# Loading wo in 112 partitions, with the last four heads' rows in small loads of their own, in a decode kernel with a 1 GB cache

## The chip, the cores and the metric

The kernel runs on one core of a Trainium2 chip. The metric is the device time of one execution in microseconds (us). A profile of one execution goes with it; its span is counted from the first to the last instruction, and the time of that same execution is a little longer than the span.

## The reference, cut to what matters

One token `x` of 512 numbers goes through attention over a cache of 65,536 positions with 32 heads of 128, and through a small gated network; a gate `g` mixes the two.

```python
q = (x @ wq).reshape(B, Sq, H, Dh).transpose(0, 2, 1, 3)          # H = 32, Dh = 128
p = softmax(einsum("bhqd,bhkd->bhqk", q, k_cache) * Dh ** -0.5)   # Sk = 65536
o = einsum("bhqk,bhkd->bhqd", p, v_cache)
a = o.transpose(0, 2, 1, 3).reshape(B, Sq, H * Dh) @ wo           # wo: 4096 x 512
b = (silu(x @ w_gate) * (x @ w_up)) @ w_down                      # w_gate: 512 x 1792
out = g * a + (1 - g) * b                                         # g = sigmoid(sum(x * gate_w))
```

All tensors are bf16. Each head's K and V take 16 MB each; `wo` takes 4 MB, 128 rows of 1 KB for each head.

## The kernel before

One big tile, `mem`, has 184 slots of 1 KB in each of 128 partitions, and nearly everything that is loaded goes through it: K and V in halves of 8 MB (64 KB in each partition), the weights at the start, and `wo` and the last head's V at the end. All large loads are issued by SP on one queue (lines 201 to 244), in an order written out by hand, each after a wait that tells that its slots are free: `ktdone` counts VectorE's transposes of K (16 for each head), `pvdone` counts TensorE's quarters of the products with V (4 for each head, ahead by 4).

For each head VectorE transposes K in 16 blocks (lines 399 and 406), TensorE multiplies them by q (line 452), ScalarE takes the exponential (line 301), VectorE rearranges the probabilities into `pb` (line 340), and TensorE multiplies them by V one head later (line 500). The result of head h is scaled and turned into column h of `oTn` (line 295), already multiplied by the gate.

The last head and the output are done apart, and this is what the change touches.

- V of head 31 comes in eight pieces, listed in `tail` (line 59): slot, first row, number of rows. The pieces have 4096, 4096, 4096, 2048, 1024, 512, 256 and 256 KB. `piece(n)` (line 506) waits for one and adds its products, with V as the stationary operand, to a column of `psW`.
- `wo` is loaded whole (line 235) into slots 64 to 95, as 128 partitions of 32 KB, each with 32 rows of `wo`. Partition p holds rows 32p to 32p + 31, a quarter of a head. Heads 0 to 30 are rearranged to fit: VectorE copies `oTn` into `amat` (line 414), one product with `bmat` (line 521) puts them into `psQ`, VectorE copies that to `oR` (line 417), and 32 products (line 526) add to the row `psY`, which already holds the gated network's result. That row is copied (line 419) and spread over four partitions of `psZ` (line 532).
- Head 31 is last. Its 128 rows of `wo` are loaded once more as 128 partitions of 1 KB (line 244), behind all of V, into slot 96 (`WO31`), when TensorE has read the last of head 30's V (`pvdone` at 4H). When `psW` is complete, VectorE writes it, scaled, on the diagonal of `w4` (line 422), and four products (line 544) add the head to `psZ`. ScalarE casts it and issues the output (lines 308 and 310).

SP's order at the end is thus: `wo`, the eight pieces (waits before pieces 0, 1 and 2), the wait for `pvdone` at 4H, head 31's rows. TensorE's order is: piece 0, the products of `wo`, piece 1, the four products into `psZ`, pieces 2 to 7, head 31's four products.

Of the kernel before, what the change touches and what calls it, by code (L numbers as in the profile page):

```python
# [5 lines left out]
P = 128  # L6
# [4 lines left out]
ALU = mybir.AluOpType  # L11
ACT = mybir.ActivationFunctionType
BF16 = mybir.dt.bfloat16
# [7 lines left out]
def bass_gated_mix__mha_block_cached__swiglu_ffn__decode_kernel(  # L21
# [13 lines left out]
    _, H, S, Dh = A_k_cache.shape  # L35
    D = A_wq.shape[0]
# [11 lines left out]
    KA, KZ, VA, VZ, V0 = 32, 0, 120, 96, 96  # L48
# [9 lines left out]

    tail = [(32, 0, 128), (0, 128, 128), (V0 + 24, 256, 128), (V0 + 64, 384, 64),
            (V0 + 80, 448, 32), (V0 + 56, 480, 16), (V0 + 60, 496, 8), (V0 + 62, 504, 8)]  # L60
    WO31 = V0

    with ExitStack() as ctx:
        def sb(name, shape, dt):
            return ctx.enter_context(nc.sbuf_tensor(name, shape, dt))
# [4 lines left out]
        def sem(name):  # L70
            return ctx.enter_context(nc.semaphore(name))
# [3 lines left out]
        psY = psum("psY", [P, 512], F32)  # L75
# [3 lines left out]
        psW = psum("psW", [P, 512], F32)  # L79
        psZ = psum("psZ", [P, 512], F32)  # L80
# [19 lines left out]
        oTn = sb("oTn", [P, H], BF16)  # L100
        amat = sb("amat", [P, H, 4], BF16)
        bmat = sb("bmat", [P, 32], BF16)
        oR = sb("oR", [P, 32], BF16)
        w4 = sb("w4", [P, 4, 4], BF16)
        fin = sb("fin", [P, 128], BF16)

        def at(kb, n):
            return mem[:, kb * KB:kb * KB + n]
# [5 lines left out]
        yrow = kt[:, 0, 0:512].bitcast(F32)  # L114
        mxs, amx, nbias, rsum, Lt, Li, LiG = (sm[:, i:i + 1] for i in range(7))

        names = ("x", "gw", "wq", "wg", "wu", "wd", "ka0", "ka", "kz", "va", "vz", "wo", "w31")
        d = {n: sem("d_" + n) for n in names}
        dt_ = [sem(f"d_t{i}") for i in range(len(tail))]
        s_ones = sem("s_ones")  # L120
# [27 lines left out]
        pvdone = sem("pvdone")  # L148
# [15 lines left out]
        s_yr = sem("s_yr")  # L164
        s_w = sem("s_w")
        s_w4 = sem("s_w4")
        s_z4 = sem("s_z4")
        s_fin = sem("s_fin")
        s_out = sem("s_out")
# [6 lines left out]
            "wg": B_w_gate.rearrange("(p c) f -> p (c f)", c=Dc),  # L176
            "wu": B_w_up.rearrange("(p c) f -> p (c f)", c=Dc),
            "wd": B_w_down.rearrange("(p c) n -> p (c n)", c=FC),
            "wo": A_wo.rearrange("(p j) n -> p (j n)", p=P),
        }  # L180
        w31_dram = A_wo.rearrange("(h d) n -> h d n", d=Dh)[H - 1]
        WQ, WG, WU, WD, WO = V0, 0, 14, V0 + 64, 64
        wq_ap = at(WQ, Dc * H * Dh).rearrange("p (c n) -> p c n", c=Dc)
        wg_ap = at(WG, Dc * F).rearrange("p (c m j) -> p c m j", c=Dc, j=FC)
        wu_ap = at(WU, Dc * F).rearrange("p (c m j) -> p c m j", c=Dc, j=FC)
        wd_ap = at(WD, FC * D).rearrange("p (c n) -> p c n", c=FC)
        wo_ap = at(WO, 32 * D).rearrange("p (j n) -> p j n", j=32)
        w31_ap = at(WO31, D).rearrange("p (c n) -> p c n", c=4)
        ktb = [kt[:, b, :].bitcast(BF16).rearrange("p (j r m e) -> p j r m e", j=2, r=NG, e=2) for b in range(2)]

        def place(kind, h, z):
# [9 lines left out]
        @block.sync  # L201
        def _(sp):
            def load(kind, h, z):
                cache = A_k_cache if kind == "k" else A_v_cache
                sp.dma_start(at(place(kind, h, z), HR * Dh), kv_dram(cache, h)[z]).then_inc(d[kind + "az"[z]], 16)

            def weights(n, kb):
                src = w_dram[n]
                sp.dma_start(at(kb, src.shape[1]), src).then_inc(d[n], 16)

            weights("wq", WQ)
            weights("wg", WG)
            weights("wu", WU)
            weights("wd", WD)
            half = HR // 2 * Dh
            for n in range(2):
                sp.dma_start(at(KA + 32 * n, half), kv_dram(A_k_cache, 0)[0][:, n * half:n * half + half]).then_inc(
                    (d["ka0"], d["ka"])[n], 16)
            sp.wait_ge(s_q, 1)
            load("k", 0, 1)  # L220
            for h in range(1, H):
                sp.wait_ge(ktdone, 2 * NP * h - 3 if h > 1 else NP)
                load("k", h, 0)
                if h == 1:
                    sp.wait_ge(ktdone, 2 * NP - 3)
                    sp.wait_ge(s_b, 1)
                else:
                    sp.wait_ge(pvdone, 4 * h - 1)
                load("v", h - 1, 0)
                sp.wait_ge(ktdone, 2 * NP * h + NP // 2)  # L230
                load("k", h, 1)
                sp.wait_ge(pvdone, 4 * h + 1)
                load("v", h - 1, 1)
            sp.wait_ge(ktdone, 2 * NP * H - NP)
            weights("wo", WO)
            src = A_v_cache[0, H - 1].rearrange("(b p r) d -> b p (r d)", b=2, p=P)
            need = {0: (ktdone, 2 * NP * H - 3), 1: (ktdone, 2 * NP * H), 2: (pvdone, 4 * H - 1)}
            for n, (kb, r0, nr) in enumerate(tail):
                if n in need:
                    sp.wait_ge(*need[n])  # L240
                b, o = divmod(r0, HR)
                sp.dma_start(at(kb, nr * Dh), src[b][:, o * Dh:(o + nr) * Dh]).then_inc(dt_[n], 16)  # L242
            sp.wait_ge(pvdone, 4 * H)
            sp.dma_start(at(WO31, D), w31_dram).then_inc(d["w31"], 16)

        @block.gpsimd
        def _(pool):
# [66 lines left out]
        def _(dve):  # L314
# [62 lines left out]
            for g in range(4):  # L377
                last = nc.vector.tensor_copy(qd[32 * g:32 * g + 32, :, :, g],
                                             psQ[32 * g:32 * g + 32, :, 0:H].rearrange("p e h -> p h e"))
# [11 lines left out]
            with nc.vector.Fori(1, H) as i:  # L391
                n = i * (2 * NP)
# [3 lines left out]
                for c, u in enumerate(k_order[0]):  # L396
                    dve.wait_ge(qkdone, n + (c - 1))  # L397
                    src = at(KA + 8 * u, PR * Dh).bitcast(U32)
# [4 lines left out]
                for c, u in enumerate(k_order[1]):  # L403
                    dve.wait_ge(qkdone, n + (NP + c - 1))  # L404
                    src = at(KZ + 8 * u, PR * Dh).bitcast(U32)
# [5 lines left out]
            link(nc.vector.tensor_tensor(LiG, Li, gcol[:, 0:1], ALU.mult))  # L411
            dve.wait_ge(s_otn, H - 1)
            for q in range(4):
                last = nc.vector.tensor_copy(amat[32 * q:32 * q + 32, 0:H - 1, q], oTn[32 * q:32 * q + 32, 0:H - 1])
            last.then_inc(s_A, 1)
            dve.wait_ge(s_R, 1)
            nc.vector.tensor_copy(oR[:], psQ[:, 0, 0:32]).then_inc(s_oR, 1)
            dve.wait_ge(s_y, 1)
            nc.vector.tensor_copy(yrow[0:1, :], psY[0:1, :]).then_inc(s_yr, 1)
            dve.wait_ge(s_w, 1)  # L420
            diag = w4[:].rearrange("p a b -> p (a b)")[:, 0:16:5]
            nc.vector.tensor_scalar(diag, psW[:, 0:1].to_broadcast([P, 4]), LiG, None, ALU.mult).then_inc(s_w4, 1)  # L422

        @block.tensor
        def _(pe):
# [3 lines left out]
            for c in range(Dc):  # L429
                last = nc.tensor.matmul(psM[:, c:c + 1], xv[:, c, :], ones[0:1, 0:1], start=True, stop=True)  # L430
# [3 lines left out]
            for h in range(H):  # L434
                for c in range(Dc):
                    last = nc.tensor.matmul(psM[:, 128 + h:129 + h], wq_ap[:, c, h * Dh:(h + 1) * Dh],  # L436
                                            xTb[:, c:c + 1], start=(c == 0), stop=(c == Dc - 1))
# [3 lines left out]
            for je in range(4):  # L441
                last = nc.tensor.matmul(psQ[:, je, 0:H], sel[:, je, :], qTb[:], start=True, stop=True)
# [28 lines left out]
            for j in range(FC):  # L471
                last = nc.tensor.matmul(psY[0:1, :], guT[:, j:j + 1], wd_ap[:, j, :],
                                        start=(j == 0), stop=False)
# [3 lines left out]
            def turn(h):  # L477
                pe.wait_ge(s_or, h)
                for i in range(4):
                    last = nc.tensor.matmul(psT[:, 0:1], orow[0:4, i * Dh:(i + 1) * Dh], unit[0:4, i:i + 1],  # L480
                                            start=(i == 0), stop=(i == 3))
                last.then_inc(s_pt, 1)

            nc.tensor.sem_inc(pvdone, 4)
            with nc.tensor.Fori(0, H) as i:
                n = i * (2 * NP)
                pe.wait_ge(s_qc, i + 1)
                for z in range(2):
# [3 lines left out]
                    with nc.tensor.If(i > 0):  # L492
# [5 lines left out]
                        for part, rows in enumerate(v_order[z]):  # L498
                            for m, r in enumerate(rows):
                                last = nc.tensor.matmul(psO[0:4, :], pb[:, 256 * z + r:256 * z + r + 4],  # L500
                                                        vt[:, r * Dh:(r + 4) * Dh],
                                                        start=(z == 0 and part == 0 and m == 0),
                                                        stop=(z == 1 and part == 1 and m == len(rows) - 1))
                            last.then_inc(pvdone, 1)

            def piece(n):
                kb, r0, nr = tail[n]
                pe.wait_ge(dt_[n], 16)
                vt = at(kb, nr * Dh)
                for r in range(nr):  # L510
                    col = r0 + r
                    last = nc.tensor.matmul(psW[:, 0:1], vt[:, r * Dh:(r + 1) * Dh], pb[:, col:col + 1],  # L512
                                            start=(col == 0), stop=(col == R - 1))
                return last

            turn(H)
            pe.wait_ge(s_pba, H)
            piece(0)
# [4 lines left out]
            pe.wait_ge(s_oR, 1)  # L523
            pe.wait_ge(d["wo"], 16)
            for j in range(32):
                last = nc.tensor.matmul(psY[0:1, :], oR[:, j:j + 1], wo_ap[:, j, :], start=False, stop=(j == 31))
            last.then_inc(s_y, 1)
            piece(1)
            pe.wait_ge(s_yr, 1)
# [1 line left out]
            for c in range(4):  # L531
                nc.tensor.matmul(psZ[0:4, 0:128], hot[0:1, c, :], yrow[0:1, 128 * c:128 * c + 128],
                                 start=(c == 0), stop=False)
            pe.wait_ge(s_pbz, H)
            piece(2)
            piece(3)
            piece(4)
            piece(5)
            piece(6)
            piece(7).then_inc(s_w, 1)  # L540
            pe.wait_ge(d["w31"], 16)
            pe.wait_ge(s_w4, 1)
            for c in range(4):
                last = nc.tensor.matmul(psZ[0:4, 0:128], w4[:, c, :], w31_ap[:, c, :], start=False, stop=(c == 3))
            last.then_inc(s_z4, 1)


# [26 lines left out]
```

## Time and profile before

| what | value |
|---|---|
| median of 3 runs | 2522.39 us (2521.6 to 2522.61) |
| the profiled execution: time, span | 2522.26 us, 2520.4 us |
| read from HBM | 1087.77 MB, 432 GB/s over the span |
| TensorE matmul, VectorE, ScalarE busy | 64%, 55%, 3% |
| mean granted TensorE clock | 0.705 |

The span is counted in us from the first instruction. A line of the timeline has the start, the length, the engine, the line of the kernel, the operation, its output and inputs, and in brackets the idle time before it with what ended it. A line of the DMA issues has the destination and source, how many, KB each, and the us from issue to landing (the median, where there are several). The windows give, for a stretch of the span, its length, the busy time of TensorE, its weight loads, VectorE, ScalarE and GpSimd, and then the granted clock, the mean busy share of the 16 DMA engines and GB/s.

The end of the span, load by load, from the DMA issues asked for one at a time:

| load | KB | issued | to landing | landed |
|---|---|---|---|---|
| V of head 30, second half | 8192 | 2441.00 | 27.1 | 2468.1 |
| wo | 4096 | 2441.37 | 36.5 | 2477.9 |
| piece 0 | 4096 | 2460.00 | 27.6 | 2487.6 |
| piece 1 | 4096 | 2466.58 | 30.8 | 2497.4 |
| piece 2 | 4096 | 2478.48 | 28.6 | 2507.1 |
| piece 3 | 2048 | 2478.85 | 33.1 | 2511.95 |
| piece 4 | 1024 | 2479.32 | 35.2 | 2514.5 |
| piece 5 | 512 | 2479.80 | 36.0 | 2515.8 |
| piece 6 | 256 | 2480.27 | 36.1 | 2516.4 |
| piece 7 | 256 | 2480.75 | 36.3 | 2517.05 |
| head 31's rows of wo | 128 | 2483.66 | 33.7 | 2517.4 |

Around them TensorE computes piece 0 from 2487.69, the product with `bmat` at 2491.07, the 32 products of `wo` from 2491.54 (8.80 us), piece 1 from 2500.28 (3.36 us), and piece 2 from 2507.25 (3.55 us), after 2.65 us of idle time. VectorE copies `amat` from 2487.98 (four copies, 0.82 us) and `oR` at 2491.30.

### The profile page before, as it was taken

The numbers are of one execution on the slowest core, as the hardware profiler recorded it, in microseconds if no ns is written. First come the engines' busy times: TensorE is split into PE (matmuls) and PEld (weight loads), VectorE is DVE, ScalarE is ACT, GpSimd is POOL, SyncE is SP. The second block draws the span as 40 slices with busy tenths as digits, with TensorE's granted clock in tenths as the row PEclk, the third lists the DMA queues.
The fourth block names the chain that finished last, engine by engine and source line by source line (L and its number), as shares of the span: only waits on it lengthen the run. The fifth ranks groups of instructions, "written<-read, shape, count | busy, mean of one in ns | idle before, by whom it ended". The sixth has DMA issues, their size and how long they took to land.

```text
span 2520.4 us, 46416 instructions
## 1 busy us (share of the span) xinstructions
PE 1608.1 (64%) x21429; PEld 919.9 (37%) x21429; DVE 1398.1 (55%) x1629; ACT 65.6 (3%) x195; POOL 27.0 (1%) x83
## 2 busy tenths in 40 slices
PE   3566756657667566566675665766756657657667
PEld 3333333333333333333333333333333333333334
DVE  3765564554655645546556556465464564654653
ACT  0000000000000000000000000000000000000000
POOL 0000000000000000000000000000000000000000
PEclk8567767677677676776776767767767767677677
DMA  9999999999999999999999999999999999999999
GB/s 418 420 433 433 433 433 433 433 433 433 438 437 436 434 434 433 433 435 433 433 433 433 433 433 433 433 433 433 433 433 435 437 438 434 433 433 434 433 434 388
DMA packets 20332, 1088.00 MB, mean 432 GB/s; under 512 B 2266, under 2 KB 2396, under 8 KB 2780
## 3 DMA queue, kind: packets, MB, share of 16 engines
q1 hardware_dynamic: 20304, 1087.78, 99.9%
q8 instruction: 11, 0.18, 0.0%
q14 instruction: 5, 0.04, 0.0%
q10 hardware_dynamic: 12, 0.00, 0.0%
HBM read 1087.77 MB, written 0.00 MB: 432 GB/s over the span
## 4 chain that ended last, share of the span: by engine, by line
DMA 73%; DVE 14%; issue 11%; PE 1%; DVEq 0%; SPq 0%; ACT 0%; POOL 0%
DMA mem<-in_A_k_cache_dram 70%; DVE kt L406 7%; DVE kt L399 6%; DMA mem<-in_A_v_cache_dram 3%; PE psO L500 1%; DVE kt L331 1%; DMA mem<-in_A_wq_dram 1%; PE psM L436 0%; DVE pb L340 0%; DVEq L404 0%; SPq L242 0%; PE psS L452 0%; PE psT L480 0%; DVEq L397 0%; ACT pa L301 0%
## 5 line engine op out<-in xcount | busy, mean ns | idle before, releaser
L452 PE MATMUL psS<-qcur,kt 128*128 128x4 bf16 x16384 | 519.0, 167 | 863.7 <-DVE kt L399 439.6
L500 PE MATMUL psO<-mem,pb 128*4 128x512 bf16 x3968 | 993.7, 417 | 17.9 <-DMA mem<-in_A_v_cache_dram 17.9
L406 DVE STREAM_TRANSPOSE kt<-mem 128x2048 uint32<-128x2048 uint32 x248 | 547.6, 2275 | 520.5 <-DMA mem<-in_A_k_cache_dram 520.5
L452 PEld LDWEIGHTS psS<-qcur,kt 128*128 128x128 bf16 x16384 | 476.6, 104 | 932.2 <-DVE kt L399 472.8
L399 DVE STREAM_TRANSPOSE kt<-mem 128x2048 uint32<-128x2048 uint32 x248 | 547.6, 2275 | 416.7 <-DMA mem<-in_A_k_cache_dram 416.7
L500 PEld LDWEIGHTS psO<-mem,pb 128*4 128x4 bf16 x3968 | 356.7, 91 | 626.6 <-issue 185.2
L340 DVE COPY pb<-pa 32x64 bf16<-32x64 bf16 x1024 | 235.4, 230 | 74.5 <-ACT pa L301 51.5
L480 PE MATMUL psT<-unit,orow 4*128 4x1 f32 x256 | 58.8, 347 | 0.8 <-ACT orow L293 0.8
L480 PEld LDWEIGHTS psT<-unit,orow 4*128 4x128 f32 x256 | 56.1, 319 | 1.8 <-ACT orow L293 1.3
L331 DVE STREAM_TRANSPOSE kt<-mem 128x2048 uint32<-128x2048 uint32 x16 | 35.4, 2278 | 17.3 <-DMA mem<-in_A_k_cache_dram 17.3
L345 DVE TENSOR_REDUCE sm<-psS 128x1 f32<-128x512 f32 x32 | 22.1, 692 | 35.5 <-PE psS L452 35.5
L299 ACT ACTIVATE sm<-sm 128x1 f32<-128x1 f32 x32 | 6.5, 203 | 1244.7 <-POOL sm L272 1244.7
L272 POOL PARTITION_ALL_REDUCE sm<-sm x32 | 11.3, 353 | 2393.4 <-DVE sm L345 2393.4
L293 ACT ACTIVATE orow<-psO,sm 4x512 f32<-4x512 f32 x31 | 21.0, 678 | 447.1 <-issue 447.1
L295 ACT ACTIVATE oTn<-psT,gcol 128x1 bf16<-128x1 f32 x31 | 8.2, 264 | 699.4 <-PE psT L480 699.4
L301 ACT ACTIVATE pa<-psS,sm 128x512 bf16<-128x512 f32 x32 | 22.0, 687 | 1.0
L512 PE MATMUL psW<-pb,mem 128*128 128x1 bf16 x512 | 14.6, 165 | 7.3 <-DMA mem<-in_A_v_cache_dram 6.4
L512 PEld LDWEIGHTS psW<-pb,mem 128*128 128x128 bf16 x512 | 14.0, 102 | 8.5 <-issue 6.4
L274 POOL PARTITION_ALL_REDUCE sm<-sm x32 | 12.3, 385 | 36.4 <-ACT pa L301 36.4
L436 PE MATMUL psM<-xTb,mem 128*128 128x1 bf16 x128 | 3.6, 165 | 11.0 <-DMA mem<-in_A_wq_dram 11.0
L464 PE MATMUL psM<-xTb,mem 128*128 128x1 bf16 x112 | 6.9, 198 | 4.5 <-DMA mem<-in_B_w_up_dram 4.5
L422 DVE TENSOR_SCALAR w<-psW,sm 128x4 bf16<-128x4 f32 x1 | 0.2, 227 | 16.4 <-PE psW L512 16.4
(62 smaller groups left out, 63.3 us busy)
## 6 DMA issues: line engine op xcount, KB each, us to landing
mem<-in_A_v_cache_dram SPq DMA_DIRECT2D x3, 4096.0 KB, 28.6
mem<-in_A_k_cache_dram SPq DMA_DIRECT2D x2, 4096.0 KB, 38.8
mem<-in_A_wq_dram SPq DMA_DIRECT2D x1, 4096.0 KB, 13.0
mem<-in_A_wo_dram SPq DMA_DIRECT2D x1, 4096.0 KB, 36.5
mem<-in_A_v_cache_dram SPq DMA_DIRECT2D x1, 2048.0 KB, 33.1
mem<-in_B_w_gate_dram SPq DMA_DIRECT2D x1, 1792.0 KB, 16.9
mem<-in_B_w_up_dram SPq DMA_DIRECT2D x1, 1792.0 KB, 21.2
mem<-in_B_w_down_dram SPq DMA_DIRECT2D x1, 1792.0 KB, 25.0
```

Of the source, the lines that this page charges most:

```text
L274: nc.gpsimd.partition_all_reduce(Lt, rsum, P, RADD).then_inc(s_L, 1)
L293: nc.scalar.mul(orow[0:4, :], psO[0:4, :], Li[0:4, :]).then_inc(s_or, 1)
L301: nc.scalar.activation(pa[:], psS[:], ACT.Exp, bias=nbias, scale=SCALE, accum_out=rsum).then_inc(expdone, 1)
L331: nc.vector.transpose(kt[:, i % 2, :].rearrange("p (j r t) -> p r j t", j=2, t=32), src.rearrange("p (r j t) -> p r j t", j=2, t=32)).then ...
L340: last = nc.vector.tensor_copy(dst, sr)
L345: nc.vector.reduce_max(mxs, psS[:], AX_X).then_inc(s_mx, 1)
L399: nc.vector.transpose(kt[:, c % 2, :].rearrange("p (j r t) -> p r j t", j=2, t=32), src.rearrange("p (r j t) -> p r j t", j=2, t=32)).then ...
L406: nc.vector.transpose(kt[:, c % 2, :].rearrange("p (j r t) -> p r j t", j=2, t=32), src.rearrange("p (r j t) -> p r j t", j=2, t=32)).then ...
L452: last = nc.tensor.matmul(psS[:, col + 4 * r:col + 4 * r + 4], ktb[c % 2][:, je // 2, r, :, je % 2], qcur[:, je, :], start=(je == 0), stop ...
L480: last = nc.tensor.matmul(psT[:, 0:1], orow[0:4, i * Dh:(i + 1) * Dh], unit[0:4, i:i + 1], start=(i == 0), stop=(i == 3))
L500: last = nc.tensor.matmul(psO[0:4, :], pb[:, 256 * z + r:256 * z + r + 4], vt[:, r * Dh:(r + 4) * Dh], start=(z == 0 and part == 0 and m = ...
L512: last = nc.tensor.matmul(psW[:, 0:1], vt[:, r * Dh:(r + 1) * Dh], pb[:, col:col + 1], start=(col == 0), stop=(col == R - 1))
```

## The change

`wo` is loaded for heads 0 to 27 only, 3584 rows, as 112 partitions of 32 KB: 3.5 MB. The rows of heads 28 to 31 come in four loads of 128 partitions of 1 KB, into slots 96 to 99. Heads 28 and 29 are loaded behind piece 3 of V, where SP now waits for `pvdone` at 4H, ahead of pieces 4 to 7; heads 30 and 31 behind piece 7. Each of the four heads is added to `psZ` by four products of its own (`fold`): heads 28 and 29 between pieces 3 and 4, heads 30 and 31 at the end. `w4` gets a diagonal for each of the four; VectorE fills three of them from `oTn`, after `amat` and before `oR`. The 32 products of `wo` run over 112 rows.

```diff
+    E = 28
+    WOE = V0
...
-        w4 = sb("w4", [P, 4, 4], BF16)
+        w4 = sb("w4", [P, H - E, 4, 4], BF16)
...
-            "wo": A_wo.rearrange("(p j) n -> p (j n)", p=P),
+            "wo": A_wo[0:E * Dh].rearrange("(p j) n -> p (j n)", j=32),
...
-        w31_dram = A_wo.rearrange("(h d) n -> h d n", d=Dh)[H - 1]
+        we_dram = A_wo.rearrange("(h d) n -> h d n", d=Dh)
...
-        wo_ap = at(WO, 32 * D).rearrange("p (j n) -> p j n", j=32)
+        wo_ap = at(WO, 32 * D)[0:4 * E].rearrange("p (j n) -> p j n", j=32)
+        we_ap = at(WOE, (H - E) * D).rearrange("p (h c n) -> p h c n", h=H - E, c=4)
...
-                sp.dma_start(at(kb, src.shape[1]), src).then_inc(d[n], 16)
+                sp.dma_start(at(kb, src.shape[1])[0:src.shape[0]], src).then_inc(d[n], 16)
...
+            def late_rows(h):
+                n = "w31" if h == H - 1 else "w30" if h == H - 2 else "we"
+                sp.dma_start(at(WOE + h - E, D), we_dram[h]).then_inc(d[n], 16)
...
                 sp.dma_start(at(kb, nr * Dh), src[b][:, o * Dh:(o + nr) * Dh]).then_inc(dt_[n], 16)
-            sp.wait_ge(pvdone, 4 * H)
-            sp.dma_start(at(WO31, D), w31_dram).then_inc(d["w31"], 16)
+                if n == 3:
+                    sp.wait_ge(pvdone, 4 * H)
+                    late_rows(E)
+                    late_rows(E + 1)
+            late_rows(H - 2)
+            late_rows(H - 1)
...
-                last = nc.vector.tensor_copy(amat[32 * q:32 * q + 32, 0:H - 1, q], oTn[32 * q:32 * q + 32, 0:H - 1])
+                last = nc.vector.tensor_copy(amat[32 * q:32 * q + 32, 0:E, q], oTn[32 * q:32 * q + 32, 0:E])
             last.then_inc(s_A, 1)
+            diag = w4[:].rearrange("p h a b -> p h (a b)")[:, :, 0:16:5]
+            for h in range(E, H - 1):
+                last = nc.vector.tensor_copy(diag[:, h - E, :], oTn[:, h:h + 1].to_broadcast([P, 4]))
+            last.then_inc(s_we, 1)
...
+            def fold(h):
+                for c in range(4):
+                    last = nc.tensor.matmul(psZ[0:4, 0:128], w4[:, h - E, c, :], we_ap[:, h - E, c, :], start=False,
+                                            stop=(h == H - 1 and c == 3))
+                return last
...
-                last = nc.tensor.matmul(psY[0:1, :], oR[:, j:j + 1], wo_ap[:, j, :], start=False, stop=(j == 31))
+                last = nc.tensor.matmul(psY[0:1, :], oR[0:4 * E, j:j + 1], wo_ap[:, j, :], start=False, stop=(j == 31))
...
             piece(3)
+            pe.wait_ge(s_we, 1)
+            pe.wait_ge(d["we"], 32)
+            fold(E)
+            fold(E + 1)
             piece(4)
...
             piece(7).then_inc(s_w, 1)
+            pe.wait_ge(d["w30"], 16)
+            fold(H - 2)
             pe.wait_ge(d["w31"], 16)
             pe.wait_ge(s_w4, 1)
-            for c in range(4):
-                last = nc.tensor.matmul(psZ[0:4, 0:128], w4[:, c, :], w31_ap[:, c, :], start=False, stop=(c == 3))
-            last.then_inc(s_z4, 1)
+            fold(H - 1).then_inc(s_z4, 1)
```

More of the change, by code (lines that the diff above doesn't have):

```diff
@@ L60, in bass_gated_mix__mha_block_cached__swiglu_ffn__decode_kernel @@
             (V0 + 80, 448, 32), (V0 + 56, 480, 16), (V0 + 60, 496, 8), (V0 + 62, 504, 8)]
-    WO31 = V0
+    E = 28
+    WOE = V0
     with ExitStack() as ctx:
@@ L115, in bass_gated_mix__mha_block_cached__swiglu_ffn__decode_kernel @@
         mxs, amx, nbias, rsum, Lt, Li, LiG = (sm[:, i:i + 1] for i in range(7))
-        names = ("x", "gw", "wq", "wg", "wu", "wd", "ka0", "ka", "kz", "va", "vz", "wo", "w31")
+        names = ("x", "gw", "wq", "wg", "wu", "wd", "ka0", "ka", "kz", "va", "vz", "wo", "we", "w30", "w31")
         d = {n: sem("d_" + n) for n in names}
@@ L166, in bass_gated_mix__mha_block_cached__swiglu_ffn__decode_kernel @@
         s_w4 = sem("s_w4")
+        s_we = sem("s_we")
         s_z4 = sem("s_z4")
@@ L186, in bass_gated_mix__mha_block_cached__swiglu_ffn__decode_kernel @@
         wd_ap = at(WD, FC * D).rearrange("p (c n) -> p c n", c=FC)
-        wo_ap = at(WO, 32 * D).rearrange("p (j n) -> p j n", j=32)
-        w31_ap = at(WO31, D).rearrange("p (c n) -> p c n", c=4)
+        wo_ap = at(WO, 32 * D)[0:4 * E].rearrange("p (j n) -> p j n", j=32)
+        we_ap = at(WOE, (H - E) * D).rearrange("p (h c n) -> p h c n", h=H - E, c=4)
         ktb = [kt[:, b, :].bitcast(BF16).rearrange("p (j r m e) -> p j r m e", j=2, r=NG, e=2) for b in range(2)]
@@ L420, in _ @@
             dve.wait_ge(s_w, 1)
-            diag = w4[:].rearrange("p a b -> p (a b)")[:, 0:16:5]
-            nc.vector.tensor_scalar(diag, psW[:, 0:1].to_broadcast([P, 4]), LiG, None, ALU.mult).then_inc(s_w4, 1)
+            nc.vector.tensor_scalar(diag[:, H - 1 - E, :], psW[:, 0:1].to_broadcast([P, 4]), LiG, None, ALU.mult).then_inc(s_w4, 1)
         @block.tensor
```

## The prediction

> **What bounds the kernel now.** I read the page first: its span, the row of the DMA engines, the queues and the chain of waits.
>
> ```profile
> span 2520.4 us, 46416 instructions
> ...
> DMA  9999999999999999999999999999999999999999
> ...
> q1 hardware_dynamic: 20304, 1087.78, 99.9%
> ...
> DMA 73%; DVE 14%; issue 11%; PE 1%; DVEq 0%; SPq 0%; ACT 0%; POOL 0%
> ```
>
> All 16 DMA engines work on SP's queue for 99.9% of the span, so the time is 1087.78 MB at 432 GB/s plus what stands behind the last byte. TensorE (64% busy) and VectorE (55%) have room. Next, the DMA issues, with the sizes and the time from issue to landing:
>
> ```profile
> mem<-in_A_v_cache_dram SPq DMA_DIRECT2D x3, 4096.0 KB, 28.6
> ...
> mem<-in_A_wq_dram SPq DMA_DIRECT2D x1, 4096.0 KB, 13.0
> mem<-in_A_wo_dram SPq DMA_DIRECT2D x1, 4096.0 KB, 36.5
> ...
> mem<-in_A_wo_dram SPq DMA_DIRECT2D x1, 128.0 KB, 33.7
> ```
>
> A load issued near the end waits some 27 us behind others. Issue plus time to landing (the table of landings above) gives when each lands: the load before wo 2468.1, wo 2477.9, the three pieces of 4096 KB 2487.6, 2497.4 and 2507.1. So 4096 KB cost 9.75 us; with 128 rows on 16 engines, eight rows each, a row of 32 KB costs an engine 9.75 / 8 = **1.22 us**. A piece of 256 KB costs about 0.62 us, the last 128 KB (rows of 1 KB) 2517.4 - 2517.05 = **0.33 us**.
>
> The timeline shows SP's issues near the end, then what follows the last piece of V:
>
> ```profile
> 2478.48 2.70 SPq L242 DMA_DIRECT2D mem<-in_A_v_cache_dram  x6
> 2483.66 0.33 SPq L244 DMA_DIRECT2D mem<-in_A_wo_dram  x1
> ```
>
> ```profile
> 2517.10 0.37 PE L512 MATMUL psW<-pb,mem 128*128 128x1 bf16 x8 [0.28 <-DMA mem<-in_A_v_cache_dram]
> 2517.51 0.23 DVE L422 TENSOR_SCALAR w<-psW,sm 128x4 bf16<-128x4 f32 x1 [16.45 <-PE psW L512]
> 2517.85 0.33 PEld L544 LDWEIGHTS psZ<-mem,w 128*4 128x4 bf16 x4 [0.47 <-DMA mem<-in_A_wo_dram]
> 2517.88 0.59 PE L544 MATMUL psZ<-mem,w 128*4 128x128 bf16 x4 [0.41 <-DVE w L422]
> 2518.50 0.26 ACT L308 CAST fin<-psZ 4x128 bf16<-4x128 f32 x1 [32.71 <-PE psZ L544]
> ```
>
> The last eight rows of V land at 2517.05; eight matmuls, VectorE's w4, four products, a cast and the output follow. The 128 KB of w31 land at 2517.4, hidden behind the eight matmuls and w4 (ready 2517.74). Last, the windows:
>
> ```profile
> 2500.00:2510.00 10.00, 7.35 (x242) 6.63 (x240) 0.68 (x1) 0.00 (x0) 0.00 (x0) 0.77 0.99 420
> ...
> 2516.00:2517.00 1.00, 0.77 (x23) 0.60 (x20) 0.00 (x0) 0.00 (x0) 0.00 (x0) 0.50 0.25 91
> ```
>
> The DMA share (last but one) falls to 0.25 a microsecond before the last piece counts as landed: most engines are done, a few are late. A load has landed when its **slowest engine** has, so the end is set by the engine with most to do, not by bytes.
>
> **The change, part by part.** The sum is made against the profiled execution: span 2520.4, time 2522.26, 0.13 below the median of 2522.39.
>
> *wo in 112 rows instead of 128.* Bytes fall by 512 KB. No load of this trace has other than 128 or 1 to 4 partitions, so its cost is bounded. Lower end: 112 = 16 x 7, every engine has one row less, -1.22 us. Upper end: all loads here give each engine the same eight rows' share of SBUF, and I don't know whether 27 GB/s (32 KB in 1.22 us) is what an engine can move or what its part of SBUF can take. If the second, seven rows per engine no longer fall into the old shares, engines meet where they write, and a row that two of them share takes 2.44 us. With m shared rows of seven on the slowest engine the load changes by (7 + m - 8) x 1.22 = (m - 1) x 1.22: -1.22 for m = 0, +7.3 for m = 7. The nearest row is the only load of this size that was not at 9.75: wq, in rows of 32 KB, 13.0, or +3.3, with the queue's start in it. The middle, m = 3.5, gives **+3.05**, which I take; both ends stay in the range. The engines behind a late one do not help it, since each works its queue in order.
>
> [...]
>
> *Rows of heads 28 to 31.* Four loads of 128 KB for one. Two go ahead of V's last four pieces: 2 x 0.33 = **+0.66** before V's end (bounds 0.60 at 432 GB/s, 1.24 if each cost as much as a piece of 256 KB). Two lie behind V: w30 lands 0.33 and w31 0.66 after it.
>
> *SP.* Pieces 4 to 7 now stand behind the wait for TensorE's last product of head 30, passed at 2483.66; before, the fourth of them was issued at 2480.75. Eight issues of some 0.47 (2.70 / 6 and the gaps) end at 2487.5. At 2483.66 the engines still have the pieces landing from 2487.6 to 2511.95 ahead of them: 28 us of cover, cost 0. If that cover were gone, 4.3 us of delay (2483.66 - 2479.32) would go straight to the end. POOL's queue isn't passed.
>
> *VectorE.* Three copies more, some 0.2 each (L414: 0.82 for four), and amat narrower: done by 2489.5, while the product that it would wait for next starts at 2491.07. Hidden by piece 0 on TensorE; uncovered, 0.6, which the 2.65 us of TensorE's idle before piece 2 would take up. The larger memset of w4 lies under the first load.
>
> *TensorE.* 32 products of wo over 112 rows: same columns, same 8.80 us. If wo lands 3 us late (2481), they start at 2491.54 as before. Heads 28 and 29: eight products, 1.2 us by the 0.59 for four, after piece 3 (64 x 0.028 = 1.8) in the 3.2 us between pieces 3 and 4 landing; hidden with 0.2 to spare, and piece 4 has another 0.35 behind it. Head 30's four start when piece 7's are done, 0.45 after V's landing, and run beside VectorE's w4; head 31's can be 0 to 0.4 later than now: **+0.2**. w31 lands 0.66 after V, w4 is ready 0.70 after it: no new wait.
>
> Sum: +3.05 + 0.66 + 0.2 = **+3.9**, so 2522.26 + 3.9 = **2526.2 us**. This kernel's runs can tell about 0.2%, 5.0 us, from no change: my forecast is no change by that mark, on the slow side of it.
>
> **The rivals.**
>
> *The seven rows run undisturbed* (m = 0): -1.22 + 0.66 + 0.2 = -0.36, **2521.9**. For it: 16 divides 112; a row costs an engine 1.22 whatever is loaded. Against it: the rate has only been seen with eight partitions to an engine.
>
> *The engines keep their old partitions*, so fourteen carry eight rows and two none: wo costs 9.75 as before, the rest +0.86, **2523.1**. The change then does not do what it says: 512 KB less, no time less. Against it: 16 divides 112.
>
> *The collisions are heavy* (slower). Place: wo's load alone, from 2468.1. Above m = 4.4 ((m - 1) x 1.22 + 0.86 = 5.0) the run is slower by over 0.2%; with all seven rows shared by two, +7.3 + 0.86 = +8.2, **2530.4**; four engines on one part would make it 7 x 4.88 - 9.75 = +24.4, 2547.5. For it: the DMA engines have no idle time to win it back, each queue runs in order, and the late engine decides every later landing. [...]
>
> **How the numbers follow.** Middling collisions (own range 2523.5 to 2528.5) 0.42, a quarter of it above 2527.4; undisturbed 0.18; old partitions 0.07; heavy 0.30; something unforeseen 0.03. Slower by over 0.2%: 0.30 + 0.11 + 0.01 = 0.42; faster by over 0.2%, for which 5 us would have to go while the change takes out 1.22 at most, 0.02; within, 0.56. The range, 2521.3 to 2533, takes in the first three cases and most of the fourth; left out are the worst collisions.
>
> **What would show it.** Landing of wo against that of the load before it: 9.75 now; 8.5 if undisturbed, about 12.8 in my forecast, 17 if all rows are shared. In the windows, a DMA share under 0.99 behind wo's issue would show engines waiting. V's last piece should land 3.7 us later, w31 0.66 behind it, and the four products of head 31 start about 1.0 us after V's landing, not 0.83. An idle stretch of the DMA engines between SP's wait and piece 4 would make the step on SP wrong; wo landing in under 9.75 would make the forecast wrong.

## The result, and the profile after

| | before | changed |
|---|---|---|
| median of 7 runs | 2522.39 us | 2530.41 us |
| lowest to highest | 2521.35 to 2522.81 | 2529.44 to 2532.51 |
| the profiled execution: time, span | 2522.26, 2520.4 | 2529.44, 2527.6 |

The changed kernel is slower: ratio 1.0032, 95% interval 1.0022 to 1.0042, or 8.0 us. That is inside the range, but beyond the mark of 0.2%, so it is the heavy rival (2530.4) that came true, not the forecast (2526.2). The profiled execution is the fastest of the seven; it shows 7.2 of the 8.0 us.

The page of the changed kernel, its span, queue, chain and DMA issues:

```profile
span 2527.6 us, 46447 instructions
...
q1 hardware_dynamic: 20720, 1087.64, 99.8%
...
DMA 73%; DVE 14%; issue 11%; PE 1%; DVEq 0%; SPq 0%; ACT 0%; POOL 0%
...
mem<-in_A_wo_dram SPq DMA_DIRECT2D x1, 3584.0 KB, 43.2
```

Fewer bytes (1087.64 MB for 1087.77), the engines as busy as before, the chain the same, and the span is 7.2 us longer. wo is an eighth smaller and lands 43.2 us after its issue, where the whole of it took 36.5.

The windows show where. A line has the stretch, its length, the busy time of TensorE, its weight loads, VectorE, ScalarE and GpSimd, the granted clock, the DMA share and GB/s. The stretches run from the landing of the load before wo to the landing of wo, and from there to that of piece 0. Before:

```profile
2468.10:2477.90 9.80, 9.72 (x39) 3.58 (x40) 3.96 (x17) 0.98 (x3) 0.74 (x2) 0.84 0.99 428
2477.90:2487.60 9.70, 6.78 (x35) 3.04 (x33) 3.70 (x17) 0.94 (x2) 0.00 (x0) 1.00 1.00 432
```

Changed:

```profile
2469.60:2484.40 14.80, 14.76 (x58) 5.38 (x59) 3.69 (x16) 0.00 (x0) 0.38 (x1) 0.83 0.99 277
2484.40:2493.80 9.40, 2.65 (x16) 1.41 (x14) 5.08 (x25) 0.94 (x2) 0.00 (x0) 0.70 1.00 432
```

While wo moves, the DMA engines are counted 0.99 busy and deliver 277 GB/s instead of 428. The moment it has landed they are back at 432. The stretch itself is 5.0 us longer, and it begins late as well: the load before wo took 28.8 us to land, for 27.1. Although it was issued 0.2 us earlier, wo lands 6.5 us later than before (2484.4 for 2477.9). Piece 3 landed at 2518.13, 6.2 later, and the last piece of V 7.25 later.

The trace also keeps, for every row that a DMA engine moved, when it began and how long it took; no view shown here prints these records, and they are put down to their loads by their size and order. In the kernel before, the 128 rows of wo took 1.21 to 1.22 us each. In the changed kernel none of the 112 was that fast: they took 1.7 to 2.6 us, 2.07 on average, and this holds for all 16 engines. The last rows of V ahead of them, 64 KB each, took up to 3.6 us; in the kernel before they took 2.42 to 2.43.

The end of the changed kernel, in the timeline:

```profile
2521.00 1.01 PE L533 MATMUL psZ<-mem,w 128*4 128x128 bf16 x8
...
2524.35 0.38 PE L527 MATMUL psW<-pb,mem 128*128 128x1 bf16 x8 [0.27 <-DMA mem<-in_A_v_cache_dram]
...
2524.69 1.03 PE L533 MATMUL psZ<-mem,w 128*4 128x128 bf16 x8
2524.77 0.23 DVE L437 TENSOR_SCALAR w<-psW,sm 128x4 bf16<-128x4 f32 x1 [17.22 <-PE psW L527]
2525.76 0.26 ACT L320 CAST fin<-psZ 4x128 bf16<-4x128 f32 x1 [37.59 <-PE psZ L533]
```

From the first product of piece 7 to the cast it takes 1.41 us, and 1.40 before (2517.10 to 2518.50): the eight products of heads 30 and 31 cost the end nothing.

### The profile page after: what moved, and what is told of

It is laid out like the page before. It is cut to its first block, busy times and chain, and to the rows that moved or that the text cites. A ratio compares the mean times of both kernels' runs of the same rounds, so it can differ in the third digit from the quotient of the medians.

```text
span 2527.6 us, 46447 instructions
## 1 busy us (share of the span) xinstructions
PE 1613.5 (64%) x21441; PEld 921.6 (36%) x21441; DVE 1398.3 (55%) x1632; ACT 65.7 (3%) x195; POOL 26.9 (1%) x83
## 3 DMA queue, kind: packets, MB, share of 16 engines
q1 hardware_dynamic: 20720, 1087.64, 99.8%
HBM read 1087.64 MB, written 0.00 MB: 430 GB/s over the span
## 4 chain that ended last, share of the span: by engine, by line
DMA 73%; DVE 14%; issue 11%; PE 1%; DVEq 0%; SPq 0%; ACT 0%; POOL 0%
DMA mem<-in_A_k_cache_dram 69%; DVE kt L418 7%; DVE kt L411 6%; DMA mem<-in_A_v_cache_dram 3%; PE psO L515 1%; DVE kt L343 1%; DMA mem<-in_A_wq_dram 0%; PE psM L451 0%; DVE pb L352 0%; DVEq L416 0%; PE psS L467 0%; PE psT L495 0%; SPq L250 0%; DVEq L409 0%; PE psZ L533 0%
## 5 line engine op out<-in xcount | busy, mean ns | idle before, releaser
L527 PE MATMUL psW<-pb,mem 128*128 128x1 bf16 x512 | 14.8, 165 | 10.9 <-DMA mem<-in_A_v_cache_dram 9.8
## 6 DMA issues: line engine op xcount, KB each, us to landing
mem<-in_A_wo_dram SPq DMA_DIRECT2D x1, 3584.0 KB, 43.2
```

## The experiments

Theory W: the engines that carry a load of other than 128 partitions write into the same parts of SBUF at the same time, and each then gets a share of that part's rate. Rival S: such a load is slow in itself, by its number of rows or by its reads. Rival R: the small loads, the moved wait and the new products cost the time. Each time stands beside runs of the kernel before on the same chip.

**One part of the change alone: wo in 112 partitions.**

```diff
-            "wo": A_wo.rearrange("(p j) n -> p (j n)", p=P),
+            "wo": A_wo[0:28 * Dh].rearrange("(p j) n -> p (j n)", j=32),
...
-                ... oR[:, j:j + 1], wo_ap[:, j, :], ...
+                ... oR[0:112, j:j + 1], wo_ap[0:112, j, :], ...
```

> The kernel before, with one edit: wo is loaded as 112 partitions of 32 KB and its 32 products run over 112 rows; heads 28 to 30 are left out of the output. Theory W (engines that write rows of 32 KB outside the 128-partition pattern meet in SBUF, and a row costs up to 2.44 us for 1.22): the load itself carries the loss, wo lands some 14.8 us behind the load before it, V's last piece 6.5 us later, time about 2528.9. Theory S (a load of seven rows an engine is slow in itself, by its reads or its shape): the same here. Rival R (the small loads, the moved wait and the new products carry the loss): wo lands 8.5 us behind the load before it and the time is 2521.2.

Measured: 2529.16 us against 2522.17, ratio 1.0027 (1.0017 to 1.0038). The window from the landing of the load before wo to that of wo:

```profile
2470.40:2484.70 14.30, 14.30 (x57) 5.25 (x58) 3.60 (x16) 0.00 (x0) 0.26 (x1) 0.85 0.97 275
```

The load alone brings 7.0 of the 8.0 us, at the 275 GB/s that the changed kernel shows. R is out as the main cause.

**That part undone: the changed kernel with wo whole.**

```diff
-            "wo": A_wo[0:E * Dh].rearrange("(p j) n -> p (j n)", j=32),
+            "wo": A_wo.rearrange("(p j) n -> p (j n)", p=P),
```

> The changed kernel with wo loaded whole again, 128 partitions of 32 KB, everything else as changed (four small loads, the moved wait, the new products). W and S: wo lands 9.75 us behind the load before it, and 3 x 0.33 less 0.1 of small loads are left: 2523.0 to 2523.3. R: 2529 to 2530, as the changed kernel.

Measured: 2523.07 us against 2522.17, ratio 1.0003 (0.9994 to 1.0012). wo lands 9.7 us behind the load before it (2467.6, 2477.3). The 0.9 us are what the sum had for the rest of the change, 0.86, but the interval does not separate them from nothing. In the profile piece 4 lands 3.3 us after piece 3 (2511.3, 2514.6), for 2.55 before: the two small loads in between, at the 0.33 each of the sum.

**The same bytes in 128 partitions.**

```diff
-            "wo": A_wo[0:E * Dh].rearrange("(p j) n -> p (j n)", j=32),
+            "wo": A_wo[0:E * Dh].rearrange("(p j) n -> p (j n)", p=P),
...
-            for j in range(32):
+            for j in range(E):
```

> The changed kernel with the same 3584 rows of wo loaded as 128 partitions of 28 KB, 28 products over 128 rows (the rows no longer meet their factors, so the output for heads 0 to 27 is another sum). W: the 128-partition pattern is back with eight rows of 28 KB an engine, no meeting; wo lands 8.5 us behind the load before it, time 2521.6 to 2522.1. S as reads or as a row length that is no power of two: a row costs more than 7/8 of 1.22 us, wo lands 10 us or more behind, time over 2523.5. R: 2529 to 2530.

Measured: 2522.36 us against 2522.17, ratio 1.0000 (0.9991 to 1.0009), a little above the 2521.6 to 2522.1 expected. wo lands 8.6 us behind the load before it:

```profile
2468.80:2477.40 8.60, 8.55 (x32) 3.08 (x33) 3.92 (x17) 0.98 (x3) 0.74 (x2) 0.79 0.99 425
```

An eighth fewer bytes take an eighth less time, 425 GB/s, as soon as all 128 partitions take part; a row of 28 KB is no obstacle. It also shows what the change could have won: the 1.2 us off wo pay for the small loads and no more, so a version with the rows of wo put right for this shape was not built.

**A power of two that isn't 128: two loads of 64 partitions.**

```diff
-            weights("wo", WO)
+            for half64 in range(2):
+                src = w_dram["wo"][64 * half64:64 * half64 + 64]
+                sp.dma_start(at(WO, src.shape[1])[64 * half64:64 * half64 + 64], src).then_inc(d["wo"], 16)
...
-            pe.wait_ge(d["wo"], 16)
+            pe.wait_ge(d["wo"], 32)
```

> The kernel before with wo (all 4 MB) loaded as two loads of 64 partitions of 32 KB, one behind the other; nothing left out. W: two loads of four rows an engine, each into half of SBUF, where engines meet in pairs: rows of 2.44 us, wo lands up to 19.5 us behind the load before it, time up to 2532.1 and at least 2528. S (seven rows an engine, or a count that is no power of two, is what is slow): four rows of 1.22 us twice, wo lands 9.8 us behind, 2522.4, no change.

Measured: 2534.13 us against 2522.17, ratio 1.0049 (1.0035 to 1.0062); 12.0 us, more than W's highest price of 9.75. The two halves land 9.7 and 19.6 us behind the load before wo, as W has it; that load is itself 2.2 us later than in the kernel before, 29.3 to landing for 27.1. The windows across wo:

```profile
2470.00:2480.00 10.00, 9.46 (x34) 3.31 (x35) 3.67 (x16) 0.00 (x0) 0.33 (x1) 0.75 1.00 210
2480.00:2490.00 10.00, 7.73 (x39) 3.43 (x37) 3.10 (x14) 0.94 (x2) 0.00 (x0) 1.00 0.91 216
2490.00:2500.00 10.00, 0.24 (x9) 0.27 (x10) 1.69 (x9) 0.00 (x0) 0.00 (x0) 0.60 1.01 436
```

The same 4 MB, the same rows of 32 KB, and half the rate throughout: 210 and 216 GB/s. A number of partitions that is no power of two isn't needed for the loss.

**The reads.** The rows of another tensor, 56 KB apart, into the same 128 partitions.

```diff
-            "wo": A_wo.rearrange("(p j) n -> p (j n)", p=P),
+            "wo": A_k_cache[0, 0, 0:P * 224].rearrange("(p r) d -> p (r d)", p=P)[:, 0:32 * D],
```

> The kernel before, with wo's load replaced by 128 rows of 32 KB out of the K cache that lie 56 KB apart, into the same 128 partitions (wo's rows for heads 0 to 30 are left out, numbers of K stand in their place). Four rows apart are then 224 KB apart, as seven rows of wo are in the changed kernel. W (the writes into SBUF meet): the writes are those of before, wo's place is filled 9.75 us behind the load before, 2522.4. Rival S', the reads from HBM are what is slow at such distances: rows of about 2 us, 14 us or more behind, 2527 or more.

Measured: 2522.40 us against 2522.16, ratio 1.0000 (0.999 to 1.001); the load lands 9.7 us behind the one before, at 432 GB/s. Rows that are read from places 56 KB apart cost nothing here.

**The place in SBUF.** Two kernels that load the same number of rows in the same shape, 2 MB, one into partitions 32 to 95 and one into 0 to 63. The edit of the first is shown; the second has 0:64 for 32:96 and stands against the first.

```diff
-            weights("wo", WO)
+            src = w_dram["wo"][32:96]
+            sp.dma_start(at(WO, src.shape[1])[32:96], src).then_inc(d["wo"], 16)
```

> The kernel before, with only 64 of wo's 128 rows of 32 KB loaded, into partitions 32 to 95 (the other 64 rows are left out; what lay in their place is multiplied). [...] If any load of 64 partitions is slow: rows of 2.55 as in the two loads of 64, landing 10.2 behind, 2522.8.

> The same with 64 rows into partitions 0 to 63 (the other 64 left out). [...] If the place does not matter: the same time as that one.

Measured, against 2522.16: partitions 32 to 95 2518.42 us, ratio 0.9983 (0.9974 to 0.9993); partitions 0 to 63 2525.34 us, ratio 1.0011 (1.0001 to 1.0020), 6.9 us apart. From the landing of the load before wo to that of wo, first the one and then the other:

```profile
2468.40:2473.30 4.90, 4.81 (x15) 1.63 (x16) 3.12 (x14) 0.98 (x3) 0.74 (x2) 0.64 0.99 428
```

```profile
2471.70:2481.50 9.80, 9.71 (x34) 3.40 (x35) 1.72 (x8) 0.00 (x0) 0.00 (x0) 0.73 0.93 227
```

428 GB/s and 227 GB/s for one shape, one size and one kind of read: where the load is written decides. That any load of 64 partitions is slow, 10.2 us behind, is excluded by the 4.9 us of the first. The rows of wo that are read differ too (32 to 95, and 0 to 63), but the two loads of 64 above read all of these at half the rate. And into partitions 32 to 95 the 64 rows go at the 428 GB/s that the 128 rows of the kernel before have. The first kernel's load takes 4.9 us less than that of the kernel before (4.90 for 9.80), but its time is only 3.7 us lower. One line of its end shows what is missing; the kernel before has the first line, this one the second:

```profile
2513.29 3.52 PE L512 MATMUL psW<-pb,mem 128*128 128x1 bf16 x108 [0.78 <-issue]
```

```profile
2510.78 3.23 PE L513 MATMUL psW<-pb,mem 128*128 128x1 bf16 x116 [1.95 <-issue]
```

Between two products of the last pieces TensorE stands for 1.95 us for nothing that the profile shows, where the kernel before has 0.78. Why is not known.

## Why the prediction was right or wrong, point by point

*What bounds the kernel.* Right: the large differences above follow from when wo lands, with TensorE and VectorE as before. Only the last 1.2 us of the 4.9 of the load into partitions 32 to 95 don't.

*wo in 112 partitions: the step that failed, by its size.* That the place of the writes decides is what the runs with one shape in two places show for 64 partitions (428 and 227 GB/s). That engines meet there is my reading of it, and for 112 partitions it is inferred from those runs and from the times of the rows. The term was taken at m = 3.5 shared rows of seven, +3.05; measured at wo's landing it is 43.2 - 36.5 = +6.7, or m = 6.5, near the upper end of +7.3. Of this 5.0 us lie in wo's own stretch (14.8 for 9.8, m = 5.1), and 1.7 in the load before it, for which the sum had nothing.

Three things made 3.5 too low. The middle was chosen between the ends for want of a row, and the row that was to support it, wq's 13.0, was a load into all 128 partitions, with the start of the queue in it; it said nothing about meeting. The sum let some of an engine's rows be shared and the others run at 1.22 us; by the records none of the 112 rows ran at 1.22, on any engine: the fastest took 1.70. Seven rows at 2.07 us on average are 14.5 us. And the loss begins before wo's own stretch, with the load of V ahead of it. It lands at 2469.6 to 2471.7 in the four kernels whose wo is slow and at 2467.6 to 2468.8 in the other five, and its slowest row takes 3.6 us in the changed kernel and 2.43 in the kernel before. (Its time from issue to landing tells less: 1.7, 2.2 and 2.7 us more than before in three of the four, but only 0.4 more with wo in 112 partitions alone, where it was issued 1.9 us later.) In the changed kernel the first row of wo begins at 2465.52 and the last of V ends at 2468.58, so engines that are done with V go on to wo while others still write V. That they slow each other by it is inferred.

That the heavy rival's price, 2530.4, is the measured time is luck in part. It was made up of +7.3 for wo and +0.86 for the rest; V's end shows 6.7 for wo, of which 0.2 go off for its earlier issue and 0.3 are won back by piece 3, and 1.1 for the small loads, 7.25 in all; the medians are 0.8 us further apart than that.

*Which engine writes what.* No run shows it: the profile does not tell the engines apart, nor where an engine writes. The runs show the rate by place alone: 428 GB/s into partitions 32 to 95, 227 into 0 to 63, 210 and 216 across the two halves one behind the other, 277 into 0 to 111 (275 with that load alone), and 425 to 432 into all 128. Why every one of the 112 rows is slowed stays open.

*Rows of heads 28 to 31.* +0.66 ahead of V's end and +0.86 in all fit the kernel with wo whole: +0.9, though not clear of nothing. In the changed kernel the two small loads cost more: piece 4 lands 3.7 us behind piece 3 (2518.1, 2521.8), some 1.1 more than before and near the upper bound of 1.24. Why isn't shown.

*SP.* The cost of 0 was right, its working was not. The eight issues were to end by 2487.5; SP's timeline has

```profile
2486.88 7.47 SPq L250 DMA_DIRECT2D mem<-in_A_v_cache_dram  x4
2494.40 16.33 SPq L243 DMA_DIRECT2D mem<-in_A_wo_dram  x2
```

and ends at 2510.7. Nothing was lost by it, for the queue held more than that ahead: head 30's rows, issued at 2494.40, landed at 2524.6, 0.3 us behind V's last.

*VectorE and TensorE.* Hidden, as worked out: the three copies took 0.31 us, not 0.6. The products of heads 28 and 29 ran for 1.01 us from 2521.00 and piece 4 followed at 2521.95, at its landing. The +0.2 at the end was 0.0.

*What would show it.* The landing of wo did; the DMA share did not. It was to fall below 0.99 and stood at 0.99 in the changed kernel's window (0.97 with that load alone, 0.93 with partitions 0 to 63): the slowed rows, 2.07 us each on average for 1.22, count as busy for as long as they take. GB/s is the column that falls (277 for 428).

*The rivals.* Undisturbed rows (2521.9) and old partitions (2523.1) are excluded by the 14.8 us that wo took, against 8.5 and 9.75; the first is what 128 partitions of 28 KB give. The heavy rival had 0.30 and should have had more than the forecast.

## What to carry to other kernels

Where loads bound the time, look first at which partitions a load covers, and then at its bytes: here an eighth fewer bytes into 112 partitions cost 7 us, and the same bytes into 128 partitions nothing. Here it was right to cut the load along its rows (28 KB instead of 32) and to keep the 128 partitions: 425 GB/s for 277. For a suspected loss of rate look at GB/s by stage, not at the busy share, and at the landing of the load before, which was late here too (2469.6 for 2468.1).

## What the runs showed of the hardware that was not expected

- With nine loads outstanding on SP's queue the issue of a tenth stood for 2.0 to 8.5 us: in the changed kernel 6.05 for piece 7, 8.45 for head 30's rows and 7.84 for head 31's; with wo whole 7.71 and 8.47 for the last two; with two loads of 64, 2.00 for head 31's. It ended near the landing of an older load, from 3.1 us ahead of it to 0.6 us behind it. In the kernel before head 31's is the ninth and took 0.33. Whether it goes by the number of loads or of their rows isn't shown.
- The rate of a 2 MB load in rows of 32 KB was 428 GB/s into partitions 32 to 95 and 227 GB/s into 0 to 63.
